# Attention with global and local keys, then a gated feed-forward: transposes of the exponentials moved from TensorE to transposing transfers in three batches, their shifted V made by copies, a fourth PSUM bank, and q and k turned elsewhere in the order

## The chip, the cores and the metric

The kernel runs on one core of one Trainium2 chip. A core has five engines that run their own instruction streams and wait for each other through semaphores: TensorE (PE in the profile, with weight loads as PEld), VectorE (DVE), ScalarE (ACT), GpSimd (POOL) and SyncE (SP). Here POOL and SP compute almost nothing: they issue transfers, POOL the loads from memory and SP all others. The metric is the device time of one execution in microseconds. The median of three runs of the kernel before is 366.84 us (365.52 to 367.23).

## The reference, cut to what matters

There are 8 batches of 8 heads. Each batch has 512 local positions and 32 global ones, and a head has 64 dimensions.

```python
k_all = concat([k_g, k_l]); v_all = concat([v_g, v_l])
out_g = softmax(scale * q_g @ k_all.T) @ v_all           # 32 global queries see all keys
mask  = abs(i - j) <= 32                                  # local queries see a band ...
s_l   = concat([scale * q_l @ k_g.T, where(mask, scale * q_l @ k_l.T, -1e9)])
out_l = softmax(s_l) @ concat([v_g, v_l])                 # ... and the 32 global keys
x     = concat([out_g, out_l]) as 4352 rows of 512 (heads side by side)
h     = x @ w_in                                          # 512 -> 2048
y     = (h * clip(h + 3, 0, 6) / 6) @ w_out               # 2048 -> 512, float32
```

## The kernel before

**Attention of a batch.** Local queries are taken in four blocks `j` of 128. For a block, `local_scores` (L246, L248) makes the scores of all 8 heads into a PSUM tile `s` of two banks: each group of 32 queries meets the 32 global keys and the 96 local keys around it, 128 columns in all. `head_max` (L255, DVE) adds the band mask and takes the maximum of a head; `head_exp` (L261, ACT) makes its exponentials, into one half of a tile `ex` of 128 x 8 x 128. The product with V contracts over keys, so the exponentials must have keys in the partitions: `turn` (L266) transposes the 8 heads on TensorE into the PSUM tile `t`, and `turn_copy` (L271, ACT) copies them to the tile `et`. `local_av` (L282) multiplies by V into `a`, `local_norm` (L297, L298, DVE) divides by the sums, and the result `x` goes transposed into `xt`: in batches 0 and 1 by TensorE (`local_x_turn`), later by a transposing transfer that SP issues (`local_x`, L304). Global queries go the same way in two halves `e`: `global_scores` (L339), `global_max` (L346), `global_exp` (L356), `turn` of 6 blocks, `turn_copy`, `global_av` (L366), `global_norm`.

**V.** A window of 96 local keys starts at any multiple of 32, and TensorE reads V from partition 0 on. So V lies three times in `vw`, shifted by 32 rows each: `v_load` brings copy 0 from memory (POOL), `spread` (L126, DVE) writes the global V into the first 32 partitions of each, and `shift` (L133 to L136) makes copies 1 and 2 of the local rows by four transfers that SP issues. Two buffers `vw` alternate between batches.

**q and k** come with positions in the partitions and are needed with dimensions there. Batches 0 to 3 are turned on TensorE (`pair_qk`, L206 and L210) and copied by ACT; batches 4 to 7 by eight transposing transfers of 128 x 512 each (`qk_turn`, L226, SP). Two buffers `qk` alternate, so batch `b` can be turned only when the scores of batch `b - 2` are done; two buffers for the loaded `qn` and `kn` alternate too.

**Feed-forward.** `first` (L397) makes 128 rows of `h` for 512 positions in 4 matmuls, into one PSUM bank of the pool `m`, which has three; `relu` (L404, ACT) and `gate` (L409, DVE) read it and write `gts`. A batch has 16 such groups. `second` (L415) makes 128 output rows with 16 matmuls in four quarters, also into a bank of `m`; ACT or DVE copies it to `ot` (L704) and SP stores it (L714). The rows of the global queries of all batches go through together at the end (`xg`, `ggs`).

PSUM is full: three banks for `m`, two for `s`, one for `t`, two for `a`.

**What sets the order.** No loop of the program sets it. Every step is an `op` with an engine, a due time `t`, an estimated cost, the ops it depends on and the buffers that it takes and ends. `lay_out` runs through them as a list scheduler: of the ops that could start on an engine it takes the one with the earliest due time, and it books the estimated cost and a lag until others may follow (for SP a `service` time of the transfer as well). The instructions are then recorded in that order, and on the chip each engine works through its own list strictly in order. `after` orders an op behind the issue of others without a wait on their results. `alt` names a second engine that may take the op. Due times are such that the attention of batch `b + 2` runs beside the feed-forward of batches `b` and `b + 1`: first the 16 first groups of a batch with blocks of the next batch's attention among them, then its four second groups with the rest of that attention.

**Names and lines for the change**: `shift` L133, `turn` L266, `turn_copy` L271, `first` L397, the class `Op`, `lay_out`, `qk_turn_ops`, `v_ops`, `local_ops`, `global_ops`, `first_ops`, `second_ops`, and the loop at the end with the due times.

Of the kernel before, what the change touches and what calls it, by code (L numbers as in the profile page):

```python
# [9 lines left out]
FP32 = mybir.dt.float32  # L10
# [4 lines left out]
def kernel(  # L15
# [113 lines left out]
    def shift(b, i0, i1):  # L129
# [6 lines left out]
        nc.sync.dma_start(out=v[64:128, 2, here, :, :], in_=v[32:96, 0, there, :, :])  # L136

    def load_w_in(k):
        n = dff // WC
        load(w_in_t[k], moe_w_in[:, k * n:(k + 1) * n].rearrange("(m p) c -> p m c", p=P))  # L140
# [128 lines left out]
    def turn_copy(ps, n, copy=nc.scalar.copy):  # L269
        et = wrk.tile([P, H, P], FP16, tag="et", name="et", bufs=3)  # L270
        copy(out=et[:, 0:n, :].rearrange("c h q -> c (h q)"), in_=ps)  # L271
        return et

    def local_av(b, j, et):
        st = state[b]
        v = vw[b % 2]
        ps = psa.tile([P, 2, 512], FP32, tag="a", name="a")
        ps = ps[:, :, 0:4 * D1].rearrange("q i (h c) -> q i h c", c=D1)
        for h in range(H):
            for s in range(NU):  # L280
                u = NU * j + s
                nc.tensor.matmul(out=ps[s * HW:(s + 1) * HW, h // 4, h % 4, 0:D + 1],  # L282
                                 lhsT=et[:, h, s * HW:(s + 1) * HW],
                                 rhs=v[:, u % 3, u // 3, h, 0:D + 1], start=True, stop=True)
        return ps
# [104 lines left out]

    def first(x, c, k):

        n = x.shape[-1]
        ps = psm.tile([P, 512], FP32, tag="m", name="m")
        for i in range(k):
# [30 lines left out]
    class Op:  # L426
        def __init__(self, eng, t, cost, f, deps, takes, service, mode, after, alt):
            self.alt = alt
            self.eng, self.t, self.cost, self.f = eng, t, cost, f
            self.deps, self.takes, self.service, self.mode = list(deps), takes, service, mode  # L430
            self.users = {}
            self.done = self.issued = None
            self.after = after
# [3 lines left out]

    def op(eng, t, cost, f, deps=(), takes=(), ends=(), service=0.0, mode=0, after=(), alt=None):

        o = Op(eng, t, cost, f, deps, takes, service, mode, list(after), alt or {})  # L440
        for pool in takes:
# [6 lines left out]
    def lay_out():  # L448
# [27 lines left out]
        while len(order) < len(ops):  # L476
# [24 lines left out]
            elif e == SP:  # L501
                start = max(now + 0.4, stores)
                both = min(max(queue - start, 0.0), 2.0 * o.service)
                stores = start + o.service + both / 2
                o.done = max(now + cost, stores) + LAG[e]
                queue += both / 2
# [46 lines left out]

    def qk_turn_ops(b, t, w):
        m = made[b]
        for j in range(NJ):
            for i in range(2):
                o = op(SP, t + (2 * j + i) * w, 1.19, lambda i=i, j=j: qk_turn(b, i, j),
                       [m["qkload"][2 * j + i]] + before(b, "scores"), ends=(("nat", m["qkload"][0]),), service=1.1,
                       after=made[b - 2]["stores"][j:j + 1])  # L560
                m["turns"].append(o)
        m["qk"] = m["turns"]
# [25 lines left out]
    def v_ops(b, t, t_spread, t_shift):  # L588
# [6 lines left out]
        m["vhalf"] = vs[0:NW // 2 + 1] + m["v"][-3:]  # L595
        cuts = (0, half, NW - 1) if b == 0 else (0, NW - 1)
        for k, (i0, i1) in enumerate(zip(cuts, cuts[1:])):
            o = op(SP, t_shift + k, 2.3, lambda i0=i0, i1=i1: shift(b, i0, i1),
# [5 lines left out]
    def local_ops(b, j, t, dt, lag):  # L604
# [6 lines left out]
        for pairs in parts:  # L611
            o = op(PE, t, 0.42 / len(parts), lambda pairs=pairs: h.update(s=local_scores(b, j, h.get("s"), pairs)),
                   (m["turns"][0:2 * j + 4] or [m["qk"][p] for p in pairs]) + [m["gt"]], takes=() if of_head else bank,
                   mode=1, after=of_head[0:1])
# [4 lines left out]
        for i in range(H):  # L619
# [3 lines left out]
            def ex(i=i):  # L623
                if "ex" not in h:
# [4 lines left out]
        t += 7 * dt + lag  # L629
        turned = op(PE, t + 0.7, 0.45, lambda: h.update(t=turn(h["ex"], H)), exps, takes=("t",),  # L630
                    ends=(("ex", exps[0]),))
        copied = op(ACT, t + 1.3, 0.9, lambda *copy: h.update(et=turn_copy(h["t"], H, *copy)), [turned],
                    takes=("et",), ends=(("t", turned),), alt={DVE: 0.8} if b == 0 else {})
        av = op(PE, t + 2.4, 0.3, lambda: h.update(a=local_av(b, j, h["et"])), [copied] + (m["vhalf"] if j == 0 else m["v"]),
# [14 lines left out]
    def global_ops(b, e, t, later=()):  # L649
# [7 lines left out]
                [mx] + (made[b - 1]["turned"][e:e + 1] if b else []), ends=(("s", scores),))  # L657
        turned = op(PE, t + 2.4, 0.34, lambda: h.update(t=turn(h["ex"], NG)), [ex], takes=("t",))
        m["turned"].append(turned)
        copied = op(ACT, t + 3.0, 0.71, lambda: h.update(et=turn_copy(h["t"], NG)), [turned], takes=("et",),  # L660
                    ends=(("t", turned),))
        av = op(PE, t + 4.0, 0.25, lambda: h.update(a=global_av(b, e, h["et"])), [copied] + m["v"],
# [4 lines left out]
        if e == 1:  # L667
            gx = op(PE, t + 6.0, 0.06, lambda: h.update(t=global_x(b)), m["gx"], takes=("t",),
                    ends=(("xgn", m["gx"][0]),))
            m["xg"] = op(DVE, t + 6.5, 0.21, lambda: global_x_copy(b, h["t"]), [gx], ends=(("t", gx),))  # L670

    def first_ops(t, w, x, key, gs, cols, deps):

        n = cols.stop - cols.start
        k = Sl // n
        for c in range(0, NDFF, k):
            h = {}
            t0 = t + c * w
            ends = [("xt", made[key]["x"][0])] if key != "g" else ()
            mm = op(PE, t0, 0.865, lambda h=h, c=c: h.update(ps=first(x()[:, :, cols], c, k)),  # L680
                    deps + [w_in[c // WC]], takes=("m",), ends=ends)
            act = op(ACT, t0 + 0.9, 0.49, lambda h=h: h.update(t1=relu(h["ps"])), [mm], takes=("t1",))

            g = op(DVE, t0 + 1.4, 0.605, lambda h=h, c=c: gate(gs[:, c:c + k, cols], h["t1"], h["ps"]),
                   [act] + (second_of.get((key - 1, c // WC), []) if key != "g" else []),
                   ends=(("m", mm), ("t1", act)))
            gates.setdefault((key, c // WC), []).append(g)

    def second_ops(t, w, key, gs, t0, store):
        h = {}  # L690
        parts = []
        for q in range(4):
            def mm(q=q):
                if q == 0:
                    h["ps"] = psm.tile([P, 512], FP32, tag="m", name="m")
                second(h["ps"], gs, t0, q)
            o = op(PE, t + q * w, 0.865, mm, gates[key, q] + [w_out[q]] + parts[-1:],
                   takes=() if q else ("m",))
            parts.append(o)
            second_of.setdefault((key, q), []).append(o)  # L700

        def out_(copy):
            h["ot"] = moew.tile([P, dm], FP32, tag="ot", name="ot")
            copy(out=h["ot"], in_=h["ps"])  # L704
        c = op(DVE, t + 4 * w, 0.61, out_, [parts[-1]], alt={ACT: 0.54}, takes=("ot",), ends=(("m", parts[0]),))
        o = op(SP, t + 4 * w + 0.5, 0.4, lambda: store(h["ot"]), [c], ends=(("ot", c),), service=1.2)
# [13 lines left out]

    TURNED = (0, 1)
    zeroed = op(DVE, -60, 0.2, lambda: nc.vector.memset(masks[1], 0.0))
    cleared = op(DVE, -59, 0.9, lambda: clear(0))
# [37 lines left out]
    for b in range(B):  # L761
# [17 lines left out]
        if n < B:  # L779
# [6 lines left out]
            if n % 2 == 0:  # L786
                g_ops([n, n + 1], t)
            if n < 4:
                qk_ops(n, t + 0.1, 1.5)
            else:  # L790
                qk_turn_ops(n, t - 8.0, 2.0)
            for j in range(NJ):
                local_ops(n, j, L + 14 + 6.0 * j, 0.68, 0.8)
            for e in range(2):
                global_ops(n, e, L + 14 + 24.0 + 3.0 * e)
        L += 32
# [34 lines left out]
```

## Time and profile before

| | us |
|---|---|
| median of three runs | 366.84 (365.52 to 367.23) |
| the profiled execution | 368.55 |
| its span, first instruction to last | 366.8 |
| mean granted clock of TensorE in it | 0.986 |
| stores of the output, SP, one of 256 KB | 2.3 from issue to landing |
| shifts of V, SP, 165 and 330 KB | 5.3 and 5.1 |
| loads of q, k (128 KB) and V (96 KB), POOL | 6.7, 7.3 and 5.2 |
| turns of q and k, SP (16 and 16) | 2.5 and 3.6 |

The profile is one execution, taken by the hardware profiler. Groups of instructions are named by line, engine and operation, then what they write and read (out<-in, partitions x elements), the count, the busy time, the mean duration of one in ns, and the idle time of the engine just before them with what ended it. The chain that ended last is followed back from the last instruction, step by step, to what released each; "SPq" is SP's queue while it issues a transfer, "DMA a<-b" a transfer in flight. The ends of pipelined matmuls are modelled, so the distance from one start to the next says more than a duration.

### The profile page before, as it was taken

How to read it: one execution, taken by the hardware profiler on the slowest of the kernel's cores; microseconds unless marked ns; L12 is line 12 of the kernel's file. 1: busy time of each engine (PE TensorE's matmuls, PEld its weight loads, DVE VectorE, ACT ScalarE, POOL GpSimd, SP SyncE). 2: the span in 40 equal slices, each digit the busy share in tenths (PEclk: the TensorE clock that was granted, in tenths of full speed). 3: DMA queues.
4: the chain of work that ended last, by engine and by line, in shares of the span. 5: the costliest groups of instructions: out<-in, count | busy, mean ns of one | idle time of the engine just before them, and what ended most of it. 6: DMA issues, size and time to landing. Idle time of an engine off the chain costs nothing.

```text
span 366.8 us, 13591 instructions
## 1 busy us (share of the span) xinstructions
PE 334.3 (91%) x5768; PEld 185.7 (51%) x5768; DVE 233.4 (64%) x845; ACT 240.0 (65%) x520; POOL 101.0 (28%) x131
## 2 busy tenths in 40 slices
PE   1558989799999789999999999979999999999995
PEld 1446864455556444454555455534555455546542
DVE  6854875558877468745994599429944795367300
ACT  1565677768898768645894689438954895457221
POOL 8913935980150932010631054010000000000000
PEclk9999999999999959999999999999999999999999
DMA  8999999999492998459999999995615211200032
GB/s 96 116 251 195 122 227 167 182 172 171 112 130 78 143 120 132 41 126 109 176 133 145 120 157 145 123 156 105 93 54 139 73 29 50 73 30 0 2 90 82
DMA packets 136045, 42.81 MB, mean 117 GB/s; under 512 B 121712, under 2 KB 129904, under 8 KB 135984
## 3 DMA queue, kind: packets, MB, share of 16 engines
q0 software_dynamic: 98224, 17.57, 66.2%
q1 hardware_dynamic: 37760, 24.38, 30.7%
q8 instruction: 45, 0.74, 0.9%
q14 instruction: 16, 0.13, 0.1%
HBM read 35.13 MB, written 8.91 MB: 120 GB/s over the span
## 4 chain that ended last, share of the span: by engine, by line
PE 77%; DMA 9%; SPq 4%; DVE 3%; issue 2%; POOL 2%; ACT 1%; POOLq 0%; ACTq 0%; DVEq 0%
PE m L397 33%; PE m L415 27%; PE t L266 5%; DMA qk<-kn 4%; SPq L226 3%; PE a L282 3%; DMA vw<-vw 2%; PE s L246 2%; PE s L248 2%; DMA xt<-x 2%; PE s L339 1%; DMA vw<-in_v_l_dram 1%; PE t L210 1%; DVE vw L126 1%; PE a L366 1%
## 5 line engine op out<-in xcount | busy, mean ns | idle before, releaser
L397 PE MATMUL m<-xt,win 128*128 128x512 f16 (+1 forms) x576 | 124.9, 365 | 2.4 <-DVE gts L409 1.4
L415 PE MATMUL m<-wout,gts 128*128 128x512 f16 x512 | 123.3, 380 | 0.0
L404 ACT ACTIVATE t<-m 128x512 f32<-128x512 f32 x136 | 81.0, 597 | 26.4 <-PE m L397 25.9
L261 ACT ACTIVATE ex<-sm,mx 128x128 f16<-128x128 f32 x256 | 85.8, 395 | 18.7 <-DVE mx L255 16.5
L409 DVE SCALAR_TENSOR_TENSOR gts<-t,m 128x512 f16<-128x512 f32 x128 | 86.1, 682 | 17.0 <-ACT t L404 16.4
L397 PEld LDWEIGHTS <-win 128*128 128x128 f16 x640 | 60.6, 100 | 51.4 <-issue 5.4
L255 DVE CUSTOM_DVE_ANT_0 sm<-s,mask 128x128 f32<-128x128 f32 x240 | 56.6, 286 | 32.2 <-PE s L248 29.1
L415 PEld LDWEIGHTS <-gts 128*128 128x128 f16 x512 | 46.0, 98 | 47.9 <-issue 0.9
L89 POOL DMA_DIRECT2D vw<-in_v_l_dram x48 | 36.1, 763 | 61.4 <-PE a L282 51.5
L271 ACT COPY et<-t 128x1024 f16<-128x1024 f16 (+1 forms) x47 | 43.9, 934 | 13.2 <-PE t L266 12.8
L704 ACT COPY ot<-m 128x512 f32<-128x512 f32 x24 | 14.0, 582 | 46.2 <-PE m L415 46.2
L89 POOL DMA_DIRECT2D qn<-in_q_l_dram x28 | 25.5, 910 | 58.3 <-PE t L210 31.3
L89 POOL DMA_DIRECT2D kn<-in_k_l_dram x28 | 25.7, 919 | 7.4 <-DMA wout<-in_moe_w_out_dram 7.0
L248 PE MATMUL s<-qk 64*32 64x96 f16 x960 | 21.3, 209 | 6.4 <-issue 3.3
L297 DVE RECIPROCAL rec<-a 128x8 f32<-128x8 f32 (+1 forms) x48 | 9.2, 191 | 27.3 <-PE a L282 13.7
L346 DVE TENSOR_REDUCE mx<-s 128x1 f32<-128x768 f32 x16 | 15.3, 955 | 17.6 <-PE s L339 17.4
L126 DVE COPY vw<-vgs 32x3168 f16<-32x3168 f16 x24 | 24.3, 1032 | 0.0
L266 PE MATMUL t<-ident,ex 128*128 128x128 f16 x256 | 22.5, 233 | 1.3 <-ACT xt L319 0.7
L246 PEld LDWEIGHTS <-qk 64*32 64x32 f16 x1024 | 15.6, 90 | 15.5 <-issue 9.4
L298 DVE TENSOR_TENSOR x<-a,rec 128x512 f16<-128x512 f32 x32 | 22.1, 692 | 1.1
L246 PE MATMUL s<-gt,qk 64*32 64x32 f16 x960 | 18.7, 185 | 3.9 <-DVE qk L217 1.6
L266 PEld LDWEIGHTS <-ex 128*128 128x128 f16 x256 | 18.0, 103 | 8.3 <-issue 1.2
(73 smaller groups left out, 249.3 us busy)
## 6 DMA issues: line engine op xcount, KB each, us to landing
out_dram<-ot SPq DMA_DIRECT2D x32, 256.0 KB, 2.3
vw<-vw SPq DMA_DIRECT2D x14, 330.0 KB, 5.1
vw<-in_v_l_dram POOLq DMA_DIRECT2D x32, 96.0 KB, 5.2
qn<-in_q_l_dram POOLq DMA_DIRECT2D x24, 128.0 KB, 6.7
kn<-in_k_l_dram POOLq DMA_DIRECT2D x24, 128.0 KB, 7.3
vw<-vw SPq DMA_DIRECT2D x14, 165.0 KB, 5.3
win<-in_moe_w_in_dram POOLq DMA_DIRECT2D x4, 512.0 KB, 16.2
wout<-in_moe_w_out_dram POOLq DMA_DIRECT2D x4, 512.0 KB, 14.8
```

The lines of the kernel that those rows point to most:

```text
L89: nc.gpsimd.dma_start(out=o, in_=i)
L126: nc.vector.tensor_copy(out=vw[b % 2][0:Sg, c, :, :, :], in_=vgs[:, b].unsqueeze(1).to_broadcast([Sg, NW, H, D1]))
L246: nc.tensor.matmul(out=o[:, 0:Sg], lhsT=lhs, rhs=gt[rows, p, gc:gc + Sg])
L248: nc.tensor.matmul(out=o[:, Sg:P], lhsT=lhs, rhs=t[rows, k0:k0 + KW])
L255: nc.vector.tensor_tensor_reduce(out=sm, in0=ps[h % 2][:, h // 2, :], in1=m, scale=-scale, scalar=3.0e38, op0=ALU.add, op1=ALU.min, accum_ ...
L261: nc.scalar.activation(out=ex[:, h, :], in_=sm, func=EXP, scale=-1.0, bias=mx)
L266: nc.tensor.matmul(out=ps[:, h * P:(h + 1) * P], lhsT=ex[:, h, :], rhs=ident, is_transpose=True)
L271: copy(out=et[:, 0:n, :].rearrange("c h q -> c (h q)"), in_=ps)
L397: nc.tensor.matmul(out=ps[:, i * n:(i + 1) * n], lhsT=w_in_t[c // WC][:, m, (c % WC + i) * P:(c % WC + i + 1) * P], rhs=x[:, m, :], start= ...
L404: nc.scalar.activation(out=t1, in_=ps, func=RELU, bias=0.5, scale=1.0 / 6.0)
L409: nc.vector.scalar_tensor_tensor(out=g, in0=t1.rearrange("f (k n) -> f k n", n=n), scalar=1.0, in1=ps.rearrange("f (k n) -> f k n", n=n), ...
L415: nc.tensor.matmul(out=ps, lhsT=gs[:, c, t0:t0 + P], rhs=w_out_t[c // WC][:, c % WC, :], start=(c == 0), stop=(c == NDFF - 1))
```

## The change

Four things are changed, all of them in the ops and the order.

1. From batch 5 on (`EDMA`), a block's exponentials are no longer turned on TensorE and copied by ACT: one transposing transfer on SP takes the whole tile `ex` (128 x 1024, or 128 x 768 for the global halves) to `et`. That is 12 local and 6 global transfers in place of 132 TensorE transposes and 18 ACT copies.
2. From batch 5 on (`COPIED`), copies 1 and 2 of V are made by 12 copies a batch of 32 partitions each, on DVE or ACT as the planner chooses, in place of the four transfers of `shift`.
3. With `t` less used, every fourth group of the feed-forward takes the bank of `t` in place of one of `m`, from the feed-forward of batch 4 on.
4. The turns of q and k of batches 4 to 7 have earlier due times and are ordered behind other ops (the stores of batch `b - 3` and the x of batch `b - 1`, in place of the stores of batch `b - 2`), k ahead of q, and a block's scores wait for one turn less. The attention of a batch is due 2 us earlier, its global halves 2 us earlier.

In the built program TensorE has 264 instructions less (a load of weights and a matmul for each transpose), DVE has 20 more (18 copies of V, 2 output copies that ACT had), ACT 2 less (18 copies of V in, 18 of turned exponentials and those 2 out), SP 6 more (18 transfers in, 12 of `shift` out), POOL as many, with the loads of q and k of batches 6 and 7 now ahead of those of V of the batch before.

```diff
+    def shift_copy(b, c, q, i0, i1, copy):
+        k = q + c - 1
+        v = vw[b % 2]
+        copy(out=v[q * HW:(q + 1) * HW, c, i0:i1, :, :],
+             in_=v[k % 3 * HW + Sg:k % 3 * HW + Sg + HW, 0, i0 + k // 3:i1 + k // 3, :, :])
...
+    def turn_by_transfer(ex, n):
+        et = wrk.tile([P, H, P], FP16, tag="et", name="et", bufs=3)
+        nc.sync.dma_start_transpose(out=et[:, 0:n, :], in_=ex.rearrange("q h c -> q (h c)"))
+        return et
...
+    def ff_tile(pool):
+        if pool == "t":
+            return pst.tile([P, 512], FP32, tag="t", name="t")
+        return psm.tile([P, 512], FP32, tag="m", name="m")
...
                 start = max(now + 0.4, stores)
                 both = min(max(queue - start, 0.0), 2.0 * o.service)
                 stores = start + o.service + both / 2
-                o.done = max(now + cost, stores) + LAG[e]
+                o.done = max(now + cost, stores) + LAG[e] + o.slack
...
     def qk_turn_ops(b, t, w):
         m = made[b]
-        for j in range(NJ):
-            for i in range(2):
-                o = op(SP, t + (2 * j + i) * w, 1.19, lambda i=i, j=j: qk_turn(b, i, j),
-                       [m["qkload"][2 * j + i]] + before(b, "scores"), ends=(("nat", m["qkload"][0]),), service=1.1,
-                       after=made[b - 2]["stores"][j:j + 1])
-                m["turns"].append(o)
+        spots = (made[b - 3]["stores"] + made[b - 1]["x"])[2:]
+        for n in range(2 * NJ):
+            j, i = n // 2, 1 - n % 2
+            k = (n + 1) // 3
+            o = op(SP, t + n * w, 1.19, lambda i=i, j=j: qk_turn(b, i, j),
+                   [m["qkload"][2 * j + i]] + before(b, "scores"), ends=(("nat", m["qkload"][0]),), service=1.1,
+                   after=spots[k:k + 1])
+            m["turns"].append(o)
         m["qk"] = m["turns"]
...
+        if b >= COPIED:
+            for i0, i1 in ((0, half), (half, NW - 1)):
+                n = (i1 - i0) * H * D1
+                for c in range(1, 3):
+                    for q in range(1, 4):
+                        m["v"].append(op(DVE, t_shift + (i0 > 0) * 4 + c + q, 0.06 + 0.00036 * n,
+                                         lambda copy, c=c, q=q, i0=i0, i1=i1: shift_copy(b, c, q, i0, i1, copy),
+                                         vs[0:i1 + 1] + free_v, alt={ACT: 0.19 + 0.0007 * n}))
...
+            cuts = ()
...
-        turned = op(PE, t + 0.7, 0.45, lambda: h.update(t=turn(h["ex"], H)), exps, takes=("t",),
-                    ends=(("ex", exps[0]),))
-        copied = op(ACT, t + 1.3, 0.9, lambda *copy: h.update(et=turn_copy(h["t"], H, *copy)), [turned],
-                    takes=("et",), ends=(("t", turned),), alt={DVE: 0.8} if b == 0 else {})
+        if b >= EDMA:
+            copied = op(SP, t - 10, 1.3, lambda: h.update(et=turn_by_transfer(h["ex"], H)), exps,
+                        takes=("et",), ends=(("ex", exps[0]),), service=2.0, slack=3.0)
+        else:
+            ...
...
+        if b >= EDMA:
+            copied = op(SP, t - 10, 1.2, lambda: h.update(et=turn_by_transfer(h["ex"], NG)), [ex],
+                        takes=("et",), service=1.5, slack=3.0)
...
+    def bank(key, i):
+        spare = key != "g" and key + 1 >= EDMA and key + 2 >= QKDMA
+        return "t" if spare and i % 4 == 3 else "m"
...
+    COPIED = 5
+    QKDMA = 4
+    EDMA = 5
...
-                qk_turn_ops(n, t - 8.0, 2.0)
+                qk_turn_ops(n, t - 20.0, 4.0)
             for j in range(NJ):
-                local_ops(n, j, L + 14 + 6.0 * j, 0.68, 0.8)
+                local_ops(n, j, L + 12 + 6.0 * j, 0.68, 0.8)
             for e in range(2):
-                global_ops(n, e, L + 14 + 24.0 + 3.0 * e)
+                global_ops(n, e, L + 36 + 3.0 * e)
```

## The prediction

> **What bounds the kernel now.** I read the page first, then the chain of work that ended last, then busy time by stage, then what the lines of the change wait for.
>
> ```profile
> PE 334.3 (91%) x5768; PEld 185.7 (51%) x5768; DVE 233.4 (64%) x845; ACT 240.0 (65%) x520; POOL 101.0 (28%) x131
> ...
> PE 77%; DMA 9%; SPq 4%; DVE 3%; issue 2%; POOL 2%; ACT 1%; POOLq 0%; ACTq 0%; DVEq 0%
> ```
>
> TensorE is busy 91% of the span and is 77% of the chain; DMA and SP's queue make 13%. The averages hide the stages. Columns below: stretch, its length, busy us of PE, PEld, DVE, ACT, POOL, granted clock, DMA share, GB/s.
>
> ```profile
> 124.80:138.10 13.30, 9.51 (x204) 4.88 (x203) 7.56 (x44) 7.71 (x20) 6.52 (x8) 0.62 2.10 123
> ...
> 208.50:227.50 19.00, 19.00 (x343) 9.57 (x341) 18.50 (x68) 17.08 (x41) 9.24 (x11) 1.00 1.30 139
> 227.50:247.70 20.20, 18.09 (x330) 9.57 (x329) 8.24 (x37) 9.62 (x21) 2.21 (x3) 1.00 1.24 140
> 247.70:265.40 17.70, 17.70 (x337) 9.00 (x336) 17.26 (x63) 16.39 (x40) 0.00 (x0) 1.00 0.58 97
> 265.40:284.40 19.00, 19.00 (x336) 9.92 (x335) 9.20 (x39) 10.12 (x23) 0.00 (x0) 1.00 0.40 99
> ```
>
> Each batch has a stage of first matmuls (208.5, 247.7) and one of second matmuls (227.5, 265.4). PE is full in both, but in the first DVE is full too (18.50 of 19.00, 17.26 of 17.70) and ACT nearly (16.39 of 17.70); in the second both are half idle. And there are places where PE stands:
>
> ```profile
> 124.86 7.79 DMA xt<-x
> 132.79 1.87 PE m L397 x4
> 134.76 3.41 PE m L397 x8
> 138.60 1.83 PE m L397 x8
> ...
> 164.02 4.93 DMA qk<-kn
> ...
> 203.31 3.29 DMA qk<-kn
> ...
> 239.99 5.75 DMA qk<-kn
> ...
> 253.48 0.55 PE t L266 x8
> ...
> 260.41 0.45 PE t L266 x8
> ```
>
> At 124.8 the first matmuls of batch 2 wait for its last transposed x; then 12 of them take 5.28 us, where eight take 1.83 at full clock. At 164, 203 and 240 the scores of the next batch wait for q and k. The last two lines are the PE turns that the change removes.
>
> **The change part by part.** PE's order in the built programs is the same until 118.85 us and moves 132 transposes out after it; no other PE work comes or goes.
>
> *Turns off PE.* 12 sets of eight (L266, local) and 6 sets of six (global). A local set takes 0.45 to 0.55 of the chain; a global one 0.34 from its start to the next start (166.69 to 167.03). 12 x 0.45 + 6 x 0.34 = 7.4; with 0.55, 8.6. PE is full in these batches, so this lies on the path: **-7.6**, from -7.4 to -8.6.
>
> [...]
>
> *Their copies off ACT.*
>
> ```profile
> L271 ACT COPY et<-t 128x1024 f16<-128x1024 f16 x31 | 31.1, 1004 | 3.9 <-PE t L266 3.6
> L271 ACT COPY et<-t 128x768 f16<-128x768 f16 x16 | 12.8, 798 | 9.3 <-PE t L266 9.2
> L126 DVE COPY vw<-vgs 32x3168 f16<-32x3168 f16 x24 | 24.3, 1032 | 0.0
> ```
>
> 12 x 1.00 + 6 x 0.80 = 16.8 us leave ACT.
>
> *V by copies.* 36 copies come in, in the built order 18 on ACT and 18 on DVE (8 of 1056 and 10 of 1584 elements). No row has this form. ACT, by the slope from 0.585 (512 elements, L319) to 1.004 (1024): 1.03 and 1.46, so 10 x 1.03 + 8 x 1.46 = 22. DVE, by proportion to L126 (0.97 for 3168): 0.32 and 0.48, so 7.4. ACT gains 5 us, DVE 7.4, over three batches. In a first stage three copies of 0.32 fall on DVE: 18.5 + 1.0 = 19.5, against PE's 19.0 less two turns, 18.1: 1.4 too much, three times 4.2 at most. DVE's lag can run over into the second stage, where it is idle, and the fourth bank lets PE run one group further ahead. Bounds 0 to +4.2, I take **+2**. The removed shifts (2.6 us of SP issue a batch) held up no PE work in these batches: 0.
>
> *The new transfers.* 18 on SP.
>
> ```profile
> L304 SPq DMA_TRANSPOSE xt<-x x24: 1189/1208/2716, 109.7 to 315.4; - x24
> ...
> DMA to landing us min/median/max: 2.3/3.7/10.3
> ```
>
> The nearest row moves 128x512. Issue of 128x1024 is between the same 1.2 and twice it, 2.4; I take 2.4 (1.8 for 128x768), as the turned blocks double. SP's queue then holds per batch 8 x 1.23 (q, k) + 4 x 1.2 (x) + 4 x 0.34 (stores) + 4 x 2.4 + 2 x 1.8 = 29 us in a period of 34; before, 18.6 in 37. It fits, but in order: a transfer waits at the head for its exponentials, and behind it stand the next x, q and k. The tightest places: from the scores of a batch's first block to its first V matmul PE has some 11 us of other work in the new order; eight exponentials take 5 to 6, then 2.4 + 1.1 to land (2.35 less 1.2 of issue): 3 us to spare. And from the last V matmuls (j=3) to the next first matmuls 5.3 us, of which normalising takes 1.2 and x 2.35: 1.7 to spare. Uncontended nothing waits: 0. If all land like the slowest row, each batch loses 5.1 at the first place (10.3 + 1.2 against 6.4) and 6.2 at the second (10.3 against 4.1): +34. The slow landings, 10.3 among them, came with eight q and k loads in flight (the one issued at 181.21 landed at 191.16); in the new order these loads are done before the turned batches begin, as their buffers come free earlier. Nearest to the median: **+1**.
>
> *q and k earlier.* Their turns now go behind batch b-3's stores and batch b-1's x, some 25 to 30 us earlier in PE's work. PE stood for them
>
> ```profile
> PE s L248 <- DMA qk<-kn: 3.1, 3, 2.1
> ```
>
> 3.1 us in three waits: **-3.1**, at worst 0.
>
> *The tail of batch 2.* From 124.8 to 138.1 PE had two scores (0.72 each), two global V products (0.30), turns (0.34 + 0.45 + 0.06) and 16 matmuls (3.46) to do: 6.35, so 6.95 is lost, partly by the clock of 0.62. In the new order the last turn of batch 2 stands before eight second matmuls, so x is ready some 1.7 us earlier (about 123.1), and batch 5's loads start 2 us later, behind the last q turn. A transposing transfer landed like the loads issued beside it: those issued 119.54, with nothing ahead, after 3.96 us; the one at 125.59 after 7.63. x would land near 127 to 128, with two q/k turns now ahead of it, and the matmuls start 4.8 us earlier; but 1.9 us of scores and a turn that filled the gap come later. Gain 2.9 and some clock. Bounds: -6.95 if all goes; +2.5 if both turns (2 x 1.25) only delay x. I take **-3.5**.
>
> *Fourth bank*: no row shows PE waiting on banks in these batches: 0.
>
> Sum: -7.6 + 2 + 1 - 3.1 - 3.5 = -11.2. The profiled execution took 368.55 (span 366.8 and 1.75 around it), so 357.3 of the kind; the median of the runs is 366.84, 1.7 below it, so **355.6**.
>
> **The rivals.** *DVE and ACT take over in the first stages.* Then the six turns there (2.7) gain nothing and half the DVE copies (3.7) come on top, in place of +2: -11.2 + 2.7 + 3.7 - 2 = -6.8, **360**. For it: DVE at 97%. Against: idle halves right after.
>
> *The tail of batch 2 is not helped*: the two q/k turns delay x: -11.2 + 3.5 + 2.5 = -5.2, **361.6**. For it: they do stand ahead on SP. Against: they are issued by about 122.6, before x is ready.
>
> *Slower: transfers land late.* One mechanism: landings of the new transfers and of x(j=3) behind each other and behind V loads on the 16 DMA engines, at three batches. Late at one of the two places, 3 x 5.1 to 3 x 6.2, and PE comes back at a low clock as after 124.8 (6.95 lost where 3.8 were idle, so up to 1.8 times): 28 for the first, 355.6 + 15 to 28 = **371 to 384**. It decides once a batch loses over 4 us. For it: median landing 3.7, not 2.35, and SP at 29 of 34. Against: the heavy loads move away.
>
> *The change does not lift PE's bound at all* is out: 132 instructions are gone from PE's order.
>
> **How the numbers follow.** Forecast 0.62 (349 to 359.5), DVE and ACT 0.13, tail 0.10, late 0.15. Low end: 366.84 - 7.6 - 3.1 - 6.95 = 349. High end 364: over the two middle cases by their unknown +2 to +4, leaving out the late case. A measurement of this kernel tells about 0.5%, 1.8 us, from no change. Faster: 0.62 + 0.13 + 0.10, less 0.03 for what ends near 366.8: 0.82; same 0.04, slower 0.14 (of the late case nearly all).
>
> **What would show it.** The group L266 down to 160 and 60 matmuls; no qk<-kn in the chain after 150; periods from batch to batch of about 34 instead of 37; the stretch behind 124.8 shorter than 13.3, clock nearer 1. Wrong, if PE waits for et or xt transfers by over 4 us a batch, if SP's issue of 128x1024 is well over 2.4, or if PE stands for gates (L409) in the first stages.

## The result, and the profile after

The changed kernel takes 361.17 us (median of 15 runs, 358.64 to 365.5) against 366.84 before: 0.986 of it, with a 95% interval of 0.9825 to 0.9895. That is 5.7 us less where 11.2 were forecast. A second measurement gave 360.03 us and 0.9854 (0.9802 to 0.9906). The profiled execution took 361.02 us, span 359.1; that of before was 368.55, 1.7 over its own median, so the two profiles differ by 7.5 us and the medians by 5.7. Ratios leave disturbed runs out and medians take all, so that the two can differ, by up to 0.9% in the first group of experiments.

The page after, its busy times and its chain of work that ended last by engine:

```profile
PE 325.6 (91%) x5636; PEld 177.5 (49%) x5636; DVE 243.6 (68%) x865; ACT 246.7 (69%) x518; POOL 102.8 (29%) x131
...
PE 52%; DMA 18%; ACT 9%; DVE 8%; POOL 7%; issue 4%; ACTq 0%; POOLq 0%
```

132 matmuls are gone. But DVE and ACT are busier than before (233.4 and 240.0), although 16.8 us of copies have left ACT, and the chain, which was 77% PE, is now half PE, with ACT and DVE in it for 17%. (13.8 of DMA's 18% are loads that ended before 81 us, ahead of everything that the change moves.)

Busy time by stage of the changed kernel, in the columns that were explained for the kernel before. The stages of first matmuls start at 207.1 and 245.1, those of second matmuls at 226.0:

```profile
124.80:138.10 13.30, 10.72 (x229) 5.42 (x230) 10.16 (x37) 8.56 (x21) 8.01 (x10) 0.87 2.23 157
...
207.10:226.00 18.90, 18.59 (x297) 8.89 (x298) 17.11 (x64) 16.49 (x36) 1.45 (x2) 1.00 0.89 129
226.00:245.10 19.10, 17.38 (x373) 8.27 (x370) 13.40 (x59) 14.46 (x31) 2.97 (x4) 1.00 0.97 117
245.10:264.00 18.90, 18.86 (x292) 8.94 (x293) 16.73 (x54) 16.60 (x35) 0.00 (x0) 1.00 0.81 131
```

Behind 124.8 PE does more and its clock is 0.87 in place of 0.62. The second stage that starts at 226.0 has 13.4 and 14.5 us of work on DVE and ACT; such stages were half idle there before.

PE's waits, with us in total, times, and the longest:

```profile
PE m L414 <- DMA xt<-x: 3.8, 3, 1.6
...
PE m L414 <- DVE gts L426: 1.7, 4, 0.6
```

No wait for qk<-kn is left (3.1 us before). Those waits were 0.8, 0.3 and 2.1 us, ahead of the first matmuls of batches 3, 4 and 5. The wait for xt<-x, which was 0.8 in all, ahead of batch 2, is now 1.6, 0.7 and 1.6 us ahead of batches 2, 4 and 5. So 3.1 us are gone there, and 2.3 have come back at the same ends of batches.

To see what PE's shorter list was worth, I took each stretch from one batch's first matmul to the next batch's, and subtracted PE's own work at the spacing of each form in the trace (0.2165 us for a matmul of 512 columns, 0.0565 for a 128x128 transpose, 0.0049 for a score, and so on). What remains is time in which PE does not run at its pace:

```
first matmuls of batch      start-1  1-2   2-3   3-4   4-5   5-6   6-7   7-end   sum
before: length               82.4   50.4  37.9  37.6  39.1  36.7  34.8  43.9
before: lost                 32.9    9.1   4.8   2.6   4.6   2.1   1.8   0.2    58.1
after: length                81.3   46.3  39.1  40.4  38.0  33.4  34.4  42.1
after: lost                  31.8    6.1   5.8   4.5   5.1   2.5   1.8   0.2    57.8
```

PE's work fell by 7.4 us and the lost time by 0.3. So the turns came out as forecast as work of PE, and all the rest of the change, forecast at -3.6, came to nothing between these two executions. By the medians it cost 1.7, since the profiled execution of before was 1.7 over its own. Batch 2's tail gained 3.0; between the first matmuls of batches 2 and 5, 3.4 were given back. The 1.1 of the first stretch lies ahead of 118.85 us, where PE's order is the same, so it belongs to the executions and not to the change.

### The profile page after: what moved, and what is told of

It reads as the page before. It is cut to its first block, busy times and chain, and to the rows that moved or that the text cites. A ratio compares the mean times of both kernels' runs of the same rounds, so it can differ in the third digit from the quotient of the medians.

```text
span 359.1 us, 13427 instructions
## 1 busy us (share of the span) xinstructions
PE 325.6 (91%) x5636; PEld 177.5 (49%) x5636; DVE 243.6 (68%) x865; ACT 246.7 (69%) x518; POOL 102.8 (29%) x131
## 4 chain that ended last, share of the span: by engine, by line
PE 52%; DMA 18%; ACT 9%; DVE 8%; POOL 7%; issue 4%; ACTq 0%; POOLq 0%
PE m L414 19%; PE m L432 19%; DMA kn<-in_k_l_dram 7%; DMA wout<-in_moe_w_out_dram 5%; DMA xt<-x 5%; DVE gts L426 4%; PE t L432 3%; ACT vw L142 3%; ACT t L421 3%; PE t L414 2%; ACT ex L268 2%; PE t L273 2%; DMA vgs<-in_v_g_dram 2%; DVE sm L262 2%; POOL vw L89 2%
## 5 line engine op out<-in xcount | busy, mean ns | idle before, releaser
L414 PE MATMUL m<-xt,win 128*128 128x512 f16 (+1 forms) x512 | 109.9, 360 | 5.9 <-DMA xt<-x 3.8
L432 PE MATMUL m<-wout,gts 128*128 128x512 f16 x448 | 108.5, 380 | 0.1
L421 ACT ACTIVATE t<-m 128x512 f32<-128x512 f32 x120 | 71.0, 597 | 27.6 <-PE m L414 26.3
L426 DVE SCALAR_TENSOR_TENSOR gts<-t,m 128x512 f16<-128x512 f32 x112 | 75.0, 682 | 16.6 <-ACT t L421 15.9
L89 POOL DMA_DIRECT2D vw<-in_v_l_dram x48 | 37.4, 792 | 45.8 <-PE a L294 14.2
L278 ACT COPY et<-t 128x1024 f16<-128x1024 f16 (+1 forms) x29 | 27.1, 933 | 8.5 <-PE t L273 8.1
L753 ACT COPY ot<-m 128x512 f32<-128x512 f32 x19 | 11.1, 585 | 26.6 <-PE m L432 26.5
L142 ACT COPY vw<-vw 32x1056 f16<-32x1056 f16 (+1 forms) x18 | 22.8, 1264 | 0.4
L262 DVE DVE_READ_ACCUMULATOR2_ANT mx<- 128x1 f32 x256 | 21.2, 83 | 0.0
```

What stands on the lines that cost most here:

```text
L89: nc.gpsimd.dma_start(out=o, in_=i)
L142: copy(out=v[q * HW:(q + 1) * HW, c, i0:i1, :, :], in_=v[k % 3 * HW + Sg:k % 3 * HW + Sg + HW, 0, i0 + k // 3:i1 + k // 3, :, :])
L262: nc.vector.tensor_tensor_reduce(out=sm, in0=ps[h % 2][:, h // 2, :], in1=m, scale=-scale, scalar=3.0e38, op0=ALU.add, op1=ALU.min, accum_ ...
L414: nc.tensor.matmul(out=ps[:, i * n:(i + 1) * n], lhsT=w_in_t[c // WC][:, m, (c % WC + i) * P:(c % WC + i + 1) * P], rhs=x[:, m, :], start= ...
L421: nc.scalar.activation(out=t1, in_=ps, func=RELU, bias=0.5, scale=1.0 / 6.0)
L426: nc.vector.scalar_tensor_tensor(out=g, in0=t1.rearrange("f (k n) -> f k n", n=n), scalar=1.0, in1=ps.rearrange("f (k n) -> f k n", n=n), ...
```

## Experiments

All are edits of the kernels shown, each timed beside the kernel before, in three groups, each on a chip of its own; medians compare best within a group. First: a1, a2, a3, a4, with 365.94 us for the kernel before. Second: c1, b1, c2, a5, with 365.00. Third: e1, e4, d1, e2, with 364.82. Each edit but b1 also makes `lay_out` draw up a new order, so more than the named part moves.

**One part undone at a time.** a1: V shifted by transfers as before.

```diff
-    COPIED = 5
+    COPIED = B
```

> The changed kernel with V of batches 5 to 7 shifted by four transfers each, as before, in place of the 36 copies on DVE and ACT. Copies theory (22.8 us of copies on ACT and 10.1 on DVE stand in queues that are full in the stages of first matmuls, so the exponentials, x and the gates come late): the copies cost what the prediction gave them or more, and this kernel is 1.5 to 4 us faster than the changed one (357 to 359.5), the first matmuls of batches 4 and 5 start 1 to 2 us earlier, and ACT's COPY on vw is gone. Contention theory (the last x of a batch lands 3 us late behind loads and other transfers): twelve more transfers on the same queues make it worse; this kernel is 0 to 3 us slower than the changed one, and the wait for xt before the first matmuls of batches 4 and 5 stays or grows.

Measured: 357.42 us (355.93 to 358.75), ratio 0.9841 (0.9782 to 0.9901); by medians it is 0.977 of the kernel before, below every one of the changed kernel's 15 runs. The first matmuls of batches 4 and 5 start at 203.3 and 241.7 in place of 207.1 and 245.1. The interval is wide and overlaps the changed kernel's; the time speaks for the copies theory, and b1 below, which keeps the order, points the same way. The waits for xt stay, 2.4 us in three: late transfers of x are not due to the copies alone.

a2: exponentials turned on PE (and so no fourth bank but in the last batch's feed-forward, for which `bank` still gives it); a3: no fourth bank; a4: q and k at their old places, with the old due times, and a block's scores waiting for one turn more, as before.

```diff
-    EDMA = 5                                              (a2)
+    EDMA = B
-        return "t" if spare and i % 4 == 3 else "m"       (a3)
+        return "m"
-        spots = (made[b - 3]["stores"] + made[b - 1]["x"])[2:]      (a4)
-            j, i = n // 2, 1 - n % 2
+            j, i = n // 2, n % 2
-                   after=spots[k:k + 1])
+                   after=made[b - 2]["stores"][j:j + 1])
...
-                qk_turn_ops(n, t - 20.0, 4.0)
+                qk_turn_ops(n, t - 8.0, 2.0)
```

> The changed kernel with the exponentials of batches 5 to 7 turned on PE and copied by ACT as before; with that the fourth bank is not used either, since its buffer is taken by the turns. If the 132 transposes are on the path as the prediction has it: 7.6 us slower than the changed kernel (368 to 370), which would put it above the kernel before, so that all else in the change would be worth nothing or a loss of 1 to 2. If the stages of first matmuls are bound by DVE and ACT, as well as PE, part of the turns' time is not on the path: only 3 to 5 us slower (364 to 366).

> The changed kernel with the feed-forward's tiles in three PSUM banks as before. The prediction gave the fourth bank 0: the same within 1 us (360 to 362). Rival: now that the gates on DVE are late, the fourth bank carries PE over them, and without it PE stands for the gates for 1.5 to 4 us more (362.5 to 365), to be seen in PE m L414 <- DVE gts L426.

> The changed kernel with the transposing transfers of q and k in their old order and at their old places, and the scores and exponentials due 2 us later as before. By the prediction's terms (3.1 us for the waits on q and k, 3.5 for the tail of batch 2) it is 3 to 6.6 us slower than the changed kernel (364 to 368), and the waits for qk<-kn at the ends of the batches are back with 3 to 5 us each. Rival: the wait for q and k has only been taken over by the wait for the last x, so the waits change their name and the time stays within 1.5 us (360 to 362.7).

Measured: a2 367.95 us, ratio 1.0147 (1.0077 to 1.0218). a3 365.74, 1.003 (0.9974 to 1.0087). a4 376.19, 1.0371 (1.0313 to 1.0429).

a2 is some 7 us slower than the changed kernel, as its first expectation had it, but a3 shows that this is not the turns alone. Without the fourth bank nearly the whole gain of the change is gone, and a2 and a3, which differ by the turns and by the bank in the last batch, are 2.2 us apart. PE's wait for the gates in a3:

```profile
PE m L414 <- DVE gts L426: 3.9, 6, 0.9
```

It was 1.7 in four waits with the fourth bank. With three the program lets PE be three groups ahead of DVE and no more; between the first matmuls of batches 4 and 6 a3 loses 6.2 and 6.2 us where a2, with the turns on PE, loses 4.2 and 4.1.

a4 missed both expectations, by 8 us and more. Where most of it went is in a4's chain, just ahead of batch 6's first matmuls:

```profile
285.36 0.57 SPq L761
285.93 0.05 issue
286.00 0.03 issue
286.02 1.22 SPq L233
...
287.34 1.22 SPq L233
...
289.27 1.22 SPq L233
...
290.61 2.00 SPq L233
...
292.71 2.55 DMA xt<-x
...
295.31 4.89 PE m L414 x12
```

The second matmuls of the batch have ended at 284.5. Then SP issues a store, four transfers of q and k, and only then the last x, for which PE waits until 295.3. DVE had finished this x at 285.86; it was issued at 292.71. At their old places the q and k transfers stand in SP's queue ahead of x, and SP, with 18 new issues, is late. This one stretch lost 15.2 us in place of 2.5.

**The copies and the turns by themselves.** c1 is the changed kernel again. b1 keeps its order and cuts each copy of V to 4 of 66 columns, so most of the shifted V of batches 5 to 7 is left out. c2 is a1 and a3 together. a5 is the kernel before with the turns by transfer and nothing else: V by transfers, three banks, old places of q and k.

```diff
-        copy(out=v[q * HW:(q + 1) * HW, c, i0:i1, :, :],                (b1)
-             in_=v[k % 3 * HW + Sg:k % 3 * HW + Sg + HW, 0, i0 + k // 3:i1 + k // 3, :, :])
+        copy(out=v[q * HW:(q + 1) * HW, c, i0:i1, :, 0:4],
+             in_=v[k % 3 * HW + Sg:k % 3 * HW + Sg + HW, 0, i0 + k // 3:i1 + k // 3, :, 0:4])
```

> The changed kernel itself once more, beside the others on one chip, as their measure. By its first measurement 0.986 of the kernel before (0.9825 to 0.9895).

> The changed kernel with each copy of V moving 4 of the 66 columns of a head; order and places of all instructions stay, and the shifted V of batches 5 to 7 is left out but for these columns. Copies theory: what the 32.9 us of copies cost on the full engines comes back without any new transfer: 2 to 4 us faster than the changed kernel, as with the shifts by transfers, and the stages from the first matmuls of batch 3 to those of batch 5 lose 2 to 4 us less. Rival (the shifts by transfers won only because the planner's order came out better, or because of another chip): within 1 us of the changed kernel.

> Three banks, and V shifted by transfers: with the first change of these two alone the time was 1.7% above the changed kernel, with the second about 1% below it. If the fourth bank is worth its 4 to 6 us only because the copies of V make the gates late, it is worth 0 to 1.5 us here, and this kernel is 2 to 4 us faster than the changed one. If the gates are late because the stages of first matmuls are full on DVE and ACT even without the copies, the bank is worth 3 to 6 us here as well, and this kernel is 0 to 3 us slower than the changed one.

> The kernel before with one part of the change: the exponentials of batches 5 to 7 turned by transfers. V by transfers, three banks, q and k at their old places. By the prediction's term for the turns alone it is 7.6 us faster than the kernel before. By what the old places of q and k cost in the changed kernel (15 us, with transfers of q and k on SP's queue ahead of x and of the exponentials) it is no faster, and up to 10 us slower; then the chain shows SPq L233 and the first matmuls of batch 6 wait for x.

Measured: c1 360.03 us, 0.9854 (0.9802 to 0.9906). b1 357.73, 0.9762 (0.9694 to 0.983). c2 358.43, 0.9815 (0.9765 to 0.9865). a5 368.41, 1.0076 (1.0033 to 1.012).

b1 differs from c1 by the length of 36 copies and by nothing in the order: 2.3 us by medians. In the profiles 2.7 us of it lie between the first matmuls of batches 3 and 5 (3.6 and 4.0 lost against 5.4 and 5.0), and 0.7 in the stretch behind. So the copies cost some 2 to 3 us with four banks. Two of b1's six runs (360.26 and 360.64) lie within c1's range, so it is the place of the lost time, where the copies stand, that makes this firm. c2 shows that the fourth bank matters mostly because of them. With the copies it is worth some 5 us (365.74 against 361.17 and 360.03), without them about 1 (358.43 against 357.42 in another group, too little to be sure of). Between the first matmuls of batches 4 and 6, where the bank is used, PE loses 4.8 us more without it in the first pair (a3 against the changed kernel) and 1.9 in the second (c2 against a1). With three banks the copies cost 7.3 us (a3 against c2, again of two groups).

a5 against c2, on the same chip, is the change's heart: the turns by transfer in both, and 10 us between them by the fourth part of the change, the places and the order of q and k with the earlier due times. The turns alone make the kernel slower, as a5's second expectation had it. The transfers et<-ex of a5, then its loads of qn, then the same two of c2; the figures behind x12 and x4 are the issue in ns (least, median, longest), then first and last start, and the landing line gives the time from issue to landing of all 18 transfers of exponentials, 6 of them et<-eg:

```profile
L283 SPq DMA_TRANSPOSE et<-ex x12: 1232/1490/4062, 211.2 to 308.1; - x12
...
DMA to landing us min/median/max: 2.5/3.7/13.0
...
L89 POOL DMA_DIRECT2D qn<-in_q_l_dram x4: 881/892/923, 211.9 to 217.1; - x4
```

```profile
L283 SPq DMA_TRANSPOSE et<-ex x12: 1242/2039/2378, 204.3 to 295.6; - x12
...
DMA to landing us min/median/max: 3.4/4.0/6.7
...
L89 POOL DMA_DIRECT2D qn<-in_q_l_dram x4: 892/904/931, 187.3 to 192.5; - x4
```

In a5 the eight loads of batch 7's q and k start at 212, in the middle of the first turned batch, and three transfers of exponentials issued beside them (217 to 227) land after 8 to 13 us. In c2 the same loads start at 187 and are over when the turned batches begin. The new order of q and k frees their buffers earlier, which sends the loads earlier.

That is one part of it. PE loses some 3 us more in a5 than in c2 in each of the three stretches from batch 4's first matmuls to batch 7's, and loads of q and k run in the first alone, where PE waits 2.4 us for an et<-ex. In the second the wait is for the last x, which stands in SP's queue behind two transfers of et<-eg (a5, timeline):

```profile
276.35 0.69 DVE L310 TENSOR_TENSOR x<-a,rec 128x512 f16<-128x512 f32 x1
...
277.73 2.55 SPq L283 DMA_TRANSPOSE et<-eg  x2
280.73 1.19 SPq L316 DMA_TRANSPOSE xt<-x  x1
...
283.25 1.02 PE L414 MATMUL m<-xt,win 128*128 128x512 f16 x4 [2.78 <-issue]
```

This x is done at 277.04, issued at 280.73 and lands 2.4 us later. In the third stretch no single wait is longer than 0.9 us. So the early q and k make the turns affordable in two ways, by what runs on the DMA engines beside them and by what stands in SP's queue; no run parts the two.

**The late last x.** e1 and e2 turn the last quarter of x of every batch on PE, as batches 0 and 1 do with all of x; e2 turns batch 4's exponentials by transfer as well, and with `EDMA` the fourth bank starts a batch earlier too; d1 does only the latter two; e4 cuts the loads of V of batches 5 to 7 to one head of eight (the others' values are left out). All have V by transfers and four banks.

```diff
-        if b in TURNED:                          (e1, e2)
+        if b in TURNED or j == NJ - 1:
-    EDMA = 5                                     (d1, e2)
+    EDMA = 4
-             v_l[b, :, p0:p1, :].rearrange("h s d -> s h d"))       (e4)
+             v_l[b, 0:n, p0:p1, :].rearrange("h s d -> s h d"))
```

> The changed kernel with V by transfers (0.984 of the kernel before, four banks) and the last quarter of x of each batch from 2 on turned on PE, with a copy by DVE or ACT, in place of the transposing transfer (PE gets 24 transposes, 1.4 us in all). If the late landing of this transfer (5.5 us in place of the 2.35 of an idle queue) holds the first matmuls up: the waits for xt<-x before them (1.5 us a time, three or four times) go to under 0.5, and this kernel is 2 to 4 us faster than that with the shifts alone (0.973 to 0.979 of the kernel before). Rival: x itself is late, as ACT and DVE are, and the turn on PE then waits for DVE's x and moves the stand: within 1 us (0.981 to 0.987).

> The changed kernel with V by transfers, and the loads of V of batches 5 to 7 cut to one head of eight (the other heads' values are left out). If the loads of V that run beside the last x's transfer are what makes it land late: it lands within 2.4 to 3.5 us for batches 4 and 5, their waits for xt<-x are under 0.5 us, and the kernel is 1 to 3 us faster than with the shifts alone. Rival: the transfer is late because of the transposing transfers and shifts in its own queue: landings stay at 4 to 5.5 us and the time within 1 us.

> The changed kernel with V by transfers and the exponentials of batch 4 turned by transfers as well (44 transposes, 2.5 us of PE, and 5.6 us of copies on ACT less). By PE's floor: 2 to 2.5 us faster than with the shifts alone (0.977 of the kernel before). Rival: in batch 4's stages the loads still run, the six transfers land late and make the products with V or the first matmuls late: no faster, or up to 3 us slower.

> Both of these edits: if they are independent and each worth 2 to 4 us, about 0.967 to 0.972 of the kernel before (353 to 355 us). If the waits only change places, as the waits of q and k did for those of xt, 0.98 or above.

Measured: e1 355.75 us (354.7 to 357.04), 0.9753 (0.972 to 0.9785). e4 353.53, 0.9675 (0.9633 to 0.9717). d1 367.9, 1.0101 (1.0066 to 1.0137). e2 357.18, 0.9798 (0.9755 to 0.9841).

e1 is the fastest kernel of the study that leaves nothing out, 1.7 us by medians below a1, from which it differs by this alone (in another group; 2 to 4 were expected): the waits for xt<-x before first matmuls are gone, PE loses 3.8 us between the first matmuls of batches 1 and 2 (a1: 6.1), 3.1 in the next (5.2) and 2.2 (2.9). From batch 4 on it gives 3.4 of these 5.2 us back; why was not tested, but the turn and its copy fall there on engines that the trace of the changed kernel shows nearly full (from 207.1 to 226.0 PE 18.59, DVE 17.11 and ACT 16.49 of 18.90 us).

In e4, without most of V's loads, the time is some 4 us less (353.53 against a1's 357.42; its six runs spread from 350.98 to 358.2), but not in the way expected. The transfer of x before batch 4's first matmuls still took 6.4 us to land, against the 2.4 to 3.5 expected; most of what was won lies between the first matmuls of batches 2 and 3 (36.1 us in place of 38.6), where a stop of PE in the middle of a group of scores is gone. More on that stop at the end.

d1 is the same step as the change, turns and bank, one batch earlier, and loses 10 us to a1, where at most 3 were expected. Loads still run in batch 4: two transfers of x, issued at 198 and 202, landed 8.4 and 10.0 us later, and two of the exponentials, issued at 191 and 197, after 7.0 and 8.3. In the same stretch PE stopped for 5.3 us as told at the end; it went on at 212.87, 0.4 us after the later x had landed, so what each cost can't be told apart. Together with e1's edit (e2) these 10 us are recovered, but nothing more: e2 is 1.4 us behind e1, and its ratio of 0.9798 lies next to its second expectation (0.98 or above).

Left open: the new order of q and k in the kernel before with the turns still on PE, and e1's edit in batches 2 to 4 alone, which the stages make look best, were not measured; a1 was measured once.

## Why the prediction was right and wrong

*Turns off PE, -7.6: right as PE's work, wrong as a term of its own.* PE's floor fell by 7.4. But the turns by transfer alone (a5) gave +3.4 by medians (368.41 against 365.00). It takes the early q and k, and with the V copies the fourth bank too, for the 7.4 to reach the time. The prediction added terms that do not simply add. The same turns by transfer stand in a5, above the kernel before (1.0076), and in c2, below it (0.9815); with batch 4's turns and an earlier fourth bank added, d1 took 367.9 against a1's 357.42. What decided in these runs was what else was on the DMA engines and in SP's queue, not the price of a transpose (0.0565 us of PE in the trace of the changed kernel).

*Copies of V, +2: right, a little small.* Their rows in the changed kernel:

```profile
L142 ACT COPY vw<-vw 32x1584 f16<-32x1584 f16 x8 | 12.1, 1508 | 0.2
...
L142 ACT COPY vw<-vw 32x1056 f16<-32x1056 f16 x10 | 10.7, 1069 | 0.2
...
L142 DVE COPY vw<-vw 32x1584 f16<-32x1584 f16 x10 | 6.5, 654 | 0.2
...
L142 DVE COPY vw<-vw 32x1056 f16<-32x1056 f16 x8 | 3.6, 450 | 0.2
```

1.07 and 1.51 us on ACT, where 1.03 and 1.46 were worked out; 0.45 and 0.65 on DVE, where proportion gave 0.32 and 0.48, as it leaves out the part that does not shrink with the copy: by the line through the medians of the two sizes, 0.43 and 0.57, an estimate of 0.15 us. Four of the 18 took longer, 0.60 to 0.88. Together 32.9 us, and some 2 to 3 on the path. The prediction looked for it on DVE, which gates the first matmuls. The trace shows a second place, ACT's own queue (timeline; the bracket is the idle time before):

```profile
188.58 0.85 ACT L368 ACTIVATE eg<-s,nm 128x480 f16<-128x480 f32 x2
189.46 3.04 ACT L142 COPY vw<-vw 32x1584 f16<-32x1584 f16 x2
192.53 0.59 ACT L201 COPY gt<-t 128x512 f16<-128x512 f16 x1
193.81 1.01 ACT L278 COPY et<-t 128x1024 f16<-128x1024 f16 x1 [0.69 <-PE t L273]
```

Both copies are on the chain that ended last: two copies of batch 5's V take 3 us in front of the copy of gt, for whose bank batch 4's next turn waits (the bracket of L278, which waits for that turn), and with it the product with V and x. Batch 5's V is needed only in the next batch; x is needed at once.

*New transfers, +1: the issue was mis-sized, to the good.* The changed kernel's transfers of exponentials, with the landing of all 18:

```profile
L283 SPq DMA_TRANSPOSE et<-ex x12: 1231/1234/2107, 203.7 to 299.9; - x12
L283 SPq DMA_TRANSPOSE et<-eg x6: 1211/1230/1247, 232.9 to 308.6; - x6
...
DMA to landing us min/median/max: 2.5/3.1/5.4
```

The issue of 128x1024 is 1.23 us, that of 128x512; the 2.4 of the prediction was wrong for this kernel. PE never waited for et, as forecast for the first tight place. The claim that q's and k's loads are done before the turned batches begin holds, and a5 shows what it is worth.

*q and k earlier, -3.1: the step that failed.* The waits for qk<-kn are gone, and beside the turns by transfer the order is worth far more than 3.1 (10 us, c2 against a5); what it is worth with the turns on PE was not measured. But of the 3.1 us that the term counted, 2.3 came back ahead of batches 4 and 5: PE stands instead at the second tight place that the prediction named, the last x, for which it left "1.7 to spare" at a landing of 2.35. From the chain of the changed kernel:

```profile
200.88 0.69 DVE x L310
201.57 0.03 DVE sm L262
201.59 5.49 DMA xt<-x
207.09 0.05 issue
207.13 1.04 PE m L414 x4
...
239.44 5.56 DMA xt<-x
...
245.14 1.02 PE m L414 x4
```

x takes 5.5 us to land, 3.1 over the idle queue's 2.35; against 1.7 to spare, 1.4 would be lost. PE waited 0.7 us ahead of batch 4 and 1.6 ahead of batch 5, and 1.6 ahead of batch 2, where x took 5.7. The rows were there: a median landing of 3.7 and the sentence that a transposing transfer landed like the loads issued beside it. The prediction used them for a slower rival and for its +1, and kept 2.35 where it worked out what the last x has to spare. e1, which takes this transfer away, has no such wait left. The removed wait was an upper bound of a gain; how much of it was kept depended on the next one behind it.

*Tail of batch 2, -3.5: mis-sized, by as much.* The first matmuls of batch 2 started at 127.6, as forecast, but the gain was read from one execution. That stretch lost 9.1 us there, but 7.5 in both other kernels with the old order (a4 and a5), and 6.0 to 7.6 in eight with the new one (a1 to a3, c1, b1, c2, d1, e4). So 1.6 of the forecast gain belonged to the execution that was profiled, and the change gave about 1. The sum counted these 1.6 twice, since it also took off the 1.7 by which that execution lay above the median.

*Fourth bank, 0: wrong.* No row of before shows PE waiting for banks in these batches, because the gates were not yet late. With the copies of V in the same queues it carries some 5 us.

*The sum.* With -7.4 for the turns, 2 to 3 for the copies, about -1 for the tail and, for q and k, -3.1 with 2.3 back, it is an estimate of -6.2 to -7.2 from these runs and stretches; the medians gave -5.7 and, in the second measurement, -5.0; what is left over is not placed.

*What was to show it.* L266, now L273, is down to 160 and 60; no qk<-kn in the chain; the stretch behind 124.8 runs at 0.87. The periods from batch to batch came out at 39.1, 40.4, 38.0, 33.4 and 34.4: the last two are the 34 forecast (the last was 34.8 before, too), the three before them are where x, the copies and the loads meet. The first two rivals lie near the time, 360 (DVE and ACT take over) and 361.6 (the tail is not helped), but neither for its own reason: the waits for the gates are 1.7 us in all, and the tail gave about 1. That their times lie near is luck. The slower rival's mechanism is real: in d1 (7.0 to 10.0 us) and in a5's first turned batch (8 to 13) the new transfers, and in d1 x too, landed late beside loads. a4 shows another, x late in SP's queue (done at 285.86, issued at 292.71).

## What to carry to other kernels

A removed wait is worth no more than the wait that stands next lets through: price the next one at the landing times the trace shows under load (here 5.5 us), not at the fastest row (2.35). Moving work from the bounding engine to DMA paid here only where the loads of q and k had been moved away and the issuing queue held nothing less urgent ahead (c2 358.43 us, a5 368.41), so look first at what does both, and do that together with it. Copies that are not needed soon can hold up the next stage when they stand in a queue ahead of what it is waiting for, as 3.04 us of copies of V did on ACT. And a gain read from one profile should be looked for in a second one: an execution 1.7 us over its median had 1.6 of them in the very stretch that was to be improved.

## What was not expected of the hardware

The transposing transfer of 128x1024 is issued in the same 1.23 us as one of 128x512 and lands 0.4 us later when little else runs (2.75 against 2.35; changed kernel). Not every issue is as short: in c2 the median was 2.04, and in a5 one took 4.06 beside loads.

PE can stop in the middle of a group of matmuls with no wait for anything that the profile names. Between the first matmuls of batches 2 and 3 this happened at the same place, after the 2905th matmul, for 1.80 us in the changed kernel, 1.98 in c1, 1.52 in a1 and 1.88 in b1, for 0.61 in a2 and d1, for 0.14 in a3 and 0.12 in c2, and not at all in e4, where loads were cut. In d1 one such stop took 5.3 us. PE's waits of d1 from 160 to 260, and the queue of instruction code in the stretch 207.6 to 210 of that stop (packets, MB, share):

```profile
PE s L253 <- issue: 6.6, 2, 5.3
```

```profile
q8 instruction: 1, 0.02, 3.1%
```

The stop lasted from 207.59 to 212.87; one 16 KB packet of code started in it, none from 204 to 207.6. In c1, whose stop lasted from 162.1 to 164.1, such a packet started between 160 and 162.2. Three earlier stops lie 128 matmuls apart, in the changed kernel and in that before alike (after the 861st, 989th and 1117th; 0.63, 0.90 and 0.97 us in the changed kernel). The traces say more: in all fourteen, after each such stop of over 0.1 us that came later than 50 us (61 in all), PE went on 1.2 to 1.7 us after the end of the last 16 KB packet on this queue, however long it had stood. In the changed kernel the packet took from 162.77 to 164.37 and PE went on at 165.69; in d1 209.97 to 211.17 and 212.87; in c2, with a stop of 0.12, 162.21 to 163.21 and 164.58. From a distance so nearly constant I infer that PE waited for its code, and that the end of the packet sets the length of the stop; no trace names such a wait. That the packet is late because of the data on the same DMA engines would fit, and so would e4's gain; that part was not tested by a run of its own, and a3 and c2 hardly stop with no load cut.
